# Halving the contraction of the responses' argument products: pairs of 64 rows in two banks instead of full products

## The chip, the cores and the metric

The kernel runs on one core of a Trainium2 chip. The metric is the device time of one execution in microseconds (us), the median of the runs shown. A profile of one execution gives the start, the length and the tiles of each instruction on five engines: TensorE (PE; its weight loads are PEld), VectorE (DVE), ScalarE (ACT), GpSimd (POOL) and SyncE (SP). "Form" below is the part of the array that a product uses, rows*columns: 128*128 is the whole, 64*128 a half of the rows, 128*32 a quarter of the columns.

## The reference

Two mixers of the same input are blended by a gate. One is a diagonal state-space convolution (L = 2048, D = 640, N = 128), the other a two-dimensional Fourier filter:

```python
dt = jnp.exp(log_dt)
A = -jnp.exp(log_A_real) + 1j * A_imag
C = (C_real + 1j * C_imag) * dt[:, None]
P = jnp.exp((A * dt[:, None])[:, :, None] * pos[None, None, :])
K = 2.0 * jnp.einsum("dn,dnl->dl", C, P).real
y = irfft(rfft(u) * rfft(K))[:L] + u * D_skip
b = irfft2(rfft2(x) * W)
g = sigmoid((x * gate_w).sum(-1))
out = g * y + (1 - g) * b
```

The change lies in the way to K, the convolution's response: 640 channels x 2048 positions, each a sum over 128 modes.

## The kernel before, in words

A position is split as l = 64 j + a, so that exp(A dt l) is a product of one factor for j (32 values) and one for a (64 values). Then K of a channel is a small matrix product over the 128 modes. The exponents and the angles of these factors (their "arguments") are linear in j and a, and a product makes them out of the parameters and a table.

`phase_p` (L233) prepares four parameters per channel and mode, each split into two float32r parts, and stores them as 8 rows per channel. `phase_b` (L602) goes through 40 tiles t of 16 channels. The stationary operand `pars[t]` has 128 rows, (channel x, parameter row), and 128 columns, the modes. The moving operands are tables that hold, for channel x, numbers in that channel's 8 rows and zeros elsewhere:

- `mags(t)` (L633): three products of 512 columns with `rm` (16 channels x 96), each into a bank p_e of a pool of two; ScalarE takes the exponential of each into the tile e (L639, L641).
- `phases(t)` (L644): two products of 512 columns with `rp` (2 x 16 channels x 32) into p_p, a bank of the same pool; ScalarE rounds (L652), VectorE subtracts (L653), which leaves q.
- `trig(t)` (L656): four sines of 512 columns on ScalarE. `prods(t)` (L671): x on VectorE (L676 to L678), y on GpSimd (L681, L683).
- `kgen(t)` (L685): 32 small products in column quarters, form 128*32, into p_k, two instructions each (float32 goes through the array twice; the float32r products of `mags` and `phases` are one instruction each). K goes to memory (L706).

Tiles go in groups of five: five `mags`, then five times `phases` and `trig`; `prods` and `kgen` follow a tile behind.

`merge` (L164) interleaves phase_b with another stream by weights that each generator yields. That stream is first `phase_a` (the transforms of the input: p_s, form 128*64, L336 and L349), then the spectral branch (L445 on): transposes p_t (L503), row transforms p_d (L519, L520), p_eo (L552) and p_i (L566), all of form 128*128 except in the last, half-size step, then the first transform of K (phase_c). `phase_d` (L769) ends the kernel. The recorded instructions are ordered once more, engine by engine, by the framework's scheduler, which looks at which operands and banks it expects to be free; the built order is therefore not the written one. On the chip each engine goes through its own instructions in that built order.

At the kernel's start two products of zeros (p_w, L379) run before the first data have landed. `phase_p` issues the loads of `rm` and `rp` (L317, L318) from GpSimd's queue.

Of the kernel before, what the change touches and what calls it, by code (L numbers as in the profile page):

```python
# [25 lines left out]
MAGIC = 12582912.0  # L26
# [22 lines left out]
A_ORDER = [*range(31, -1, -1), *range(32, 64)]  # L49


def _tables():
# [27 lines left out]
    k = np.array(POS_K)  # L80
    a = np.arange(64)
# [36 lines left out]


    j = np.arange(32)  # L120
    rp = np.zeros((8, 16, 2, 16, 32))
    rm = np.zeros((8, 16, 16, 96))
    for x in range(16):
        rp[0:2, x, 0, x] = j + 0.5
        rp[0:2, x, 1, x] = 64 * j + 31.5
        rp[2:4, x, 1, x] = 1.0
        rm[4:6, x, x, 0:64] = A_ORDER
        rm[4:6, x, x, 64:96] = 64 * j
        rm[6:8, x, x, 64:96] = 1.0
    f = lambda x: np.ascontiguousarray(x, dtype=np.float32)  # L130
    return {"t_c1": f(c1), "t_w2": f(w2), "t_w3": f(w3), "t_td": f(td),
            "t_rp": f(rp.swapaxes(0, 1).reshape(128, 1024)), "t_rm": f(rm.swapaxes(0, 1).reshape(128, 1536))}


def _lay_out(u, log_a, a_i, c_r, c_i, log_dt, d_skip, w_r, w_i, gate_w):
# [49 lines left out]
def body(tc, A, out):  # L185
    nc = tc.nc
    T = Ctx()
    with ExitStack() as top:
# [24 lines left out]
        with ExitStack() as cctx:  # L213
            def left():
                with ExitStack() as ctx:
                    T.bc = ctx.enter_context(tc.tile_pool(name="b_c", reuse_waits="tile", bufs=1))
                    T.rm = T.bc.tile([128, 1536], F32R, name="rm")
                    T.rp = T.bc.tile([128, 1024], F32R, name="rp")
# [135 lines left out]
def phase_a(tc, A, T):  # L354
# [3 lines left out]
    with ExitStack() as ctx:  # L358
# [15 lines left out]

        V.memset(lg[:, :, :], 0.0)
        z = lg.rearrange("p x a -> p (x a)")
        p = ps.tile([128, 512], F32, tag="ps", name="p_w")
        for _ in range(2):
            P.matmul(p[:, :], z[:, 0:128], z, start=True, stop=True)  # L379

        def copy(dst, src):

# [219 lines left out]
def phase_b(tc, A, T, ctx):  # L602
# [29 lines left out]

    def mags(t):  # L633
        e = es[t] = ep.tile([128, 16, 96], F32, tag="e", name="e")
        ef = e.rearrange("p d i -> p (d i)")
        for c in range(0, 1536, 512):
            p = ps.tile([128, 512], F32, tag="ps", name="p_e")
            with after(T.pin):
                P.matmul(p[:, :], pars[t], rm[:, c:c + 512], start=True, stop=True)  # L639
            with after(st.trig):  # L640
                st.exp = S.activation(ef[:, c:c + 512], p[:, :], AF.Exp)  # L641
            yield 0.2

    def phases(t, r):  # L644
        q = wt.tile([128, 2, 16, 32], F32, tag="w", name="q")
        qf = q.rearrange("p v d i -> p (v d i)")
        r.q = qf
        for c in range(0, 1024, 512):
            p = ps.tile([128, 512], F32, tag="ps", name="p_p")
            P.matmul(p[:, :], pars[t], rp[:, c:c + 512], start=True, stop=True)  # L650

            S.activation(qf[:, c:c + 512], p[:, :], AF.Copy, bias=MAGIC)  # L652
            V.scalar_tensor_tensor(out=qf[:, c:c + 512], in0=qf[:, c:c + 512], scalar=MAGIC, in1=p[:, :], op0=ALU.subtract, op1=ALU.subtract)  # L653
            yield 0.22

    def trig(t, r):  # L656
# [324 lines left out]
```

## Time and profile before

| what | value |
|---|---|
| median of 3 runs | 605.09 us (603.9 to 607.54) |
| profiled execution, span from first to last instruction | 605.9 us, the only time given for it |
| share of the span: TensorE, VectorE, ScalarE, GpSimd | 89%, 82%, 60%, 43% |
| exponentials of p_e, 120 of 128x512 | 602 ns each |
| roundings of p_p, 80 of 128x512 | 591 ns each |
| subtractions of p_p on VectorE, 80 of 128x512 | 680 ns each |
| mean granted TensorE clock | 0.963 |

How to read the rows that follow. A row of the busy time by stage has the stretch, its length, then busy time and number of instructions of each engine, the mean granted clock, the DMA share and the GB/s. A row of a group has the line, the engine, the operation, what it writes and reads, the shape, and how many; behind the bar the busy time and the mean length in ns; behind the second bar the engine's idle time just before them. A row of the timeline has the start, the length (of several instructions: from the first's start to the last's end), the engine, the line, the operation and how many. Matmuls overlap in the array, so the length of one holds the way through it; what a product costs is read from the starts of what comes before and behind.

### The profile page before, as it was taken

The numbers are of one execution on the slowest core, as the hardware profiler recorded it, in microseconds if no ns is written. First come the engines' busy times: TensorE is split into PE (matmuls) and PEld (weight loads), VectorE is DVE, ScalarE is ACT, GpSimd is POOL, SyncE is SP. The second block draws the span as 40 slices with busy tenths as digits, with TensorE's granted clock in tenths as the row PEclk, the third lists the DMA queues.
The fourth block names the chain that finished last, engine by engine and source line by source line (L and its number), as shares of the span: only waits on it lengthen the run. The fifth ranks groups of instructions, "written<-read, shape, count | busy, mean of one in ns | idle before, by whom it ended". The sixth has DMA issues, their size and how long they took to land. (4 is left out here: it accounts for less than half of the span.)

```text
span 605.9 us, 16674 instructions
## 1 busy us (share of the span) xinstructions
PE 537.6 (89%) x7084; PEld 409.0 (68%) x7084; DVE 496.4 (82%) x748; ACT 364.5 (60%) x659; POOL 263.0 (43%) x246
## 2 busy tenths in 40 slices
PE   9598979988989989989889989898969999999875
PEld 7586647766766667666667676656859877787651
DVE  5971597598899998999998899879397696995965
ACT  4556775476857777899697897798712322232120
POOL 4931153054346344444515344416253447547533
PEclk9999999999979997999897999999998999999979
DMA  8777203235612321243250232006684989879767
GB/s 342 292 283 264 90 2 130 92 133 196 245 45 66 100 85 41 79 125 125 67 140 22 55 96 110 29 23 212 212 346 146 364 274 287 313 254 322 241 211 269
DMA packets 48082, 101.96 MB, mean 168 GB/s; under 512 B 3316, under 2 KB 32776, under 8 KB 46248
## 3 DMA queue, kind: packets, MB, share of 16 engines
q1 hardware_dynamic: 24888, 67.74, 32.1%
q10 hardware_dynamic: 20080, 22.52, 11.9%
q0 software_dynamic: 3040, 10.65, 5.3%
q8 instruction: 55, 0.90, 0.6%
q14 instruction: 19, 0.16, 0.1%
HBM read 60.91 MB, written 39.98 MB: 167 GB/s over the span
## 5 line engine op out<-in xcount | busy, mean ns | idle before, releaser
L349 PE MATMUL p_s<-t,w 128*64 128x160 f32 x1056 | 91.6, 311 | 11.2 <-ACT ut L383 6.0
L681 POOL TENSOR_TENSOR y<-e,sc 128x512 f32<-128x512 f32 x40 | 55.4, 1384 | 89.2 <-DVE x L676 46.7
L349 PEld LDWEIGHTS p_s<-t,w 128*64 128x64 f32 x1056 | 75.9, 137 | 22.3 <-ACT ut L383 6.6
L641 ACT ACTIVATE e<-p_e 128x512 f32<-128x512 f32 x120 | 68.6, 602 | 23.6 <-PE p_e L639 21.4
L683 POOL TENSOR_TENSOR y<-e,sc 128x512 f32<-128x512 f32 x40 | 55.5, 1388 | 44.9 <-ACT sc L667 32.0
L696 PE MATMUL p_k<-x,y 128*32 128x64 f32 x2560 | 63.0, 227 | 11.2 <-POOL y L681 6.1
L696 PEld LDWEIGHTS p_k<-x,y 128*32 128x32 f32 x2560 | 45.2, 112 | 39.6 <-issue 24.2
L552 PE MATMUL p_eo<-td,pmt 107*128 107x321 f32 x204 | 67.5, 450 | 3.9 <-ACT pmt L506 3.9
L337 ACT COPY t<-p_s 128x512 f32<-128x512 f32 x40 | 24.5, 621 | 69.0 <-PE p_s L336 45.5
L653 DVE SCALAR_TENSOR_TENSOR q<-q,p_p 128x512 f32<-128x512 f32 x80 | 53.4, 680 | 13.5 <-ACT q L652 13.3
L639 PE MATMUL p_e<-rm,par 128*128 128x512 f32 x120 | 58.9, 520 | 5.2 <-ACT e L641 3.7
L803 POOL TENSOR_TENSOR t<-ma 64x320 f32<-64x320 f32 x32 | 27.9, 873 | 64.2 <-DVE ma L798 54.8
L652 ACT ACTIVATE q<-p_p 128x512 f32<-128x512 f32 x80 | 46.4, 591 | 6.6 <-PE p_p L650 6.2
L552 PEld LDWEIGHTS p_eo<-td,pmt 107*128 107x128 f32 x204 | 37.7, 194 | 18.4 <-ACT pmt L506 6.4
L678 DVE TENSOR_TENSOR x<-e,cx 128x1024 f32<-128x1024 f32 x40 | 48.5, 1212 | 1.9 <-ACT cx L669 1.9
L817 PE MATMUL p_i<-t,w 128*64 128x160 f32 x528 | 45.1, 308 | 4.4 <-POOL t L804 3.4
L336 PE MATMUL p_s<-c,kt 128*64 128x128 f32 x640 | 44.3, 277 | 3.9 <-DVE mb L799 2.0
L336 PEld LDWEIGHTS p_s<-c,kt 128*64 128x64 f32 x640 | 39.5, 138 | 12.2 <-issue 6.9
L650 PE MATMUL p_p<-rp,par 128*128 128x512 f32 x80 | 43.3, 546 | 4.6 <-DVE q L653 4.5
L819 ACT COPY s<-p_i 128x640 f32<-128x640 f32 x32 | 21.8, 693 | 38.8 <-PE p_i L817 38.7
L817 PEld LDWEIGHTS p_i<-t,w 128*64 128x64 f32 x528 | 39.1, 141 | 8.9 <-POOL t L804 4.0
L798 DVE TENSOR_TENSOR ma<-p_s,us 128x640 f32<-128x640 f32 (+1 forms) x36 | 28.2, 784 | 20.3 <-PE p_s L349 13.3
(153 smaller groups left out, 1186.4 us busy)
## 6 DMA issues: line engine op xcount, KB each, us to landing
u_d<-ut SPq DMA_DIRECT2D x32, 320.0 KB, 3.2
us<-u_d ACTq DMA_DIRECT2D x16, 640.0 KB, 6.0
s_d<-s ACTq DMA_DIRECT2D x15, 640.0 KB, 6.7
t<-s_d SPq DMA_DIRECT2D x14, 640.0 KB, 5.7
ww<-in_w_l SPq DMA_DIRECT2D x8, 642.0 KB, 3.8
ue<-u_d SPq DMA_DIRECT2D x8, 640.0 KB, 4.1
k_d<-kt SPq DMA_DIRECT2D x4, 1280.0 KB, 8.7
kt<-k_d SPq DMA_DIRECT2D x8, 640.0 KB, 5.9
```

Of the source, the lines that this page charges most:

```text
L336: nc.tensor.matmul(p[64 * ri:64 * ri + 64, j, :], src(i + j), e1[ri], start=True, stop=True)
L349: ins = nc.tensor.matmul(p[64 * j:64 * j + 64, i, 160 * ri:160 * ri + 160], w2[:, x, 64 * ri:64 * ri + 64], t1[:, x // 2 if x < 32 else K0 ...
L552: P.matmul(p[:, :E], st.pmt[:DC, c, w, j, :], tv[:DC, w, c, :], start=c == 0, stop=c == 2)
L639: P.matmul(p[:, :], pars[t], rm[:, c:c + 512], start=True, stop=True)
L641: st.exp = S.activation(ef[:, c:c + 512], p[:, :], AF.Exp)
L652: S.activation(qf[:, c:c + 512], p[:, :], AF.Copy, bias=MAGIC)
L653: V.scalar_tensor_tensor(out=qf[:, c:c + 512], in0=qf[:, c:c + 512], scalar=MAGIC, in1=p[:, :], op0=ALU.subtract, op1=ALU.subtract)
L678: V.tensor_tensor(out=x[:, 0].rearrange("p d (h j) -> p d h j", h=2), in0=e[:, :, 0:64].rearrange("p d (h j) -> p d h j", h=2), in1=cx.uns ...
L681: ins = G.tensor_tensor(out=y[:, 1], in0=e[:, :, 64:96], in1=sc[:, 0], op=ALU.mult)
L683: G.tensor_tensor(out=y[:, 0], in0=e[:, :, 64:96], in1=sc[:, 1], op=ALU.mult)
L696: P.matmul(st.pb[32 * r:32 * r + 32, o, :], y[:, ri, 4 * qq + JR[r], :], x[:, ri, 4 * qq + JR[r], :], start=t % 2 + qq + 1 - ri == 0, stop ...
L817: T.mm = P.matmul(p[x:x + 64, i // 2, 160 * (i % 2):160 * (i % 2) + 160], T.w3[:, k0 + h + i, x:x + 64], t2[:, h + i, :], start=True, stop ...
```

## The change

The tables are cut to what half of the rows needs. Channels 0 to 7 of a tile lie in rows 0 to 63 and channels 8 to 15 in rows 64 to 127, so `rp` shrinks from 1024 to 512 columns: rows 0 to 63 hold the table of the lower channels and rows 64 to 127 that of the upper. `phases` becomes two products of 64 rows and 512 columns, one with each half of the rows, into two banks taken at the same time. `mags` becomes one such pair (512 of each half's 768 columns) and one full product of 512 columns that holds the remaining 256 of both halves. So the number of products stays, three and two a tile; 160 of the 200 now have the form 64*128. ScalarE and VectorE do the same instructions on views with two runs of 256 for those columns. The tables in memory shrink from 768 and 512 KB to 512 and 256 KB. The two products of zeros at the start become 40 small ones in the forms 64*64, 64*32 and 32*64, into three banks.

```diff
     for x in range(16):
-        rp[0:2, x, 0, x] = j + 0.5
-        rp[0:2, x, 1, x] = 64 * j + 31.5
-        rp[2:4, x, 1, x] = 1.0
-        rm[4:6, x, x, 0:64] = A_ORDER
+        rp[0:2, x, 0, x % 8] = j + 0.5
+        rp[0:2, x, 1, x % 8] = 64 * j + 31.5
+        rp[2:4, x, 1, x % 8] = 1.0
+        rm[4:6, x, x % 8, 0:64] = A_ORDER
...
+    rest = np.zeros((8, 2, 8, 2, 256))
+    for h in range(2):
+        rest[:, h, :, h] = rm[:, 8 * h:8 * h + 8, 512:]
+    rm = np.concatenate([rm[:, :, :512], rest.reshape(8, 16, 512)], 2)
...
-        p = ps.tile([128, 512], F32, tag="ps", name="p_w")
-        for _ in range(2):
-            P.matmul(p[:, :], z[:, 0:128], z, start=True, stop=True)
+        pw = [ps.tile([128, 512], F32, tag="ps", name="p_w") for _ in range(3)]
+        for k, w, n in ((64, 64, 3), (64, 32, 2), (32, 64, 2)):
+            for i in range(n):
+                for r in range(min(3, 128 // k)):
+                    for x in range(0, 128, w):
+                        a = slice(k * r, k * r + k)
+                        P.matmul(pw[r][x:x + w, 160 * i:160 * i + 160], z[a, x:x + w], z[a, 0:160], start=True, stop=True)
...
-        for c in range(0, 1536, 512):
-            p = ps.tile([128, 512], F32, tag="ps", name="p_e")
-            with after(T.pin):
-                P.matmul(p[:, :], pars[t], rm[:, c:c + 512], start=True, stop=True)
-            with after(st.trig):
-                st.exp = S.activation(ef[:, c:c + 512], p[:, :], AF.Exp)
-            yield 0.2
+        pq = [ps.tile([128, 512], F32, tag="ps", name="p_e") for _ in range(2)]
+        with after(T.pin):
+            for h in range(2):
+                x = slice(64 * h, 64 * h + 64)
+                P.matmul(pq[h][:, :], pars[t][x], rm[x, 0:512], start=True, stop=True)
+        with after(st.trig):
+            for h in range(2):
+                st.exp = S.activation(ef[:, h, 0:512], pq[h][:, :], AF.Exp)
+        yield 0.4
+        p = ps.tile([128, 512], F32, tag="ps", name="p_e")
+        P.matmul(p[:, :], pars[t], rm[:, 512:1024], start=True, stop=True)
+        with after(st.trig):
+            st.exp = S.activation(ef[:, :, 512:768], p.rearrange("p (h i) -> p h i", h=2), AF.Exp)
+        yield 0.2
...
-        for c in range(0, 1024, 512):
-            p = ps.tile([128, 512], F32, tag="ps", name="p_p")
-            P.matmul(p[:, :], pars[t], rp[:, c:c + 512], start=True, stop=True)
+        pq = [ps.tile([128, 2, 256], F32, tag="ps", name="p_p") for _ in range(2)]
+        for h in range(2):
+            x = slice(64 * h, 64 * h + 64)
+            P.matmul(pq[h].rearrange("p v i -> p (v i)"), pars[t][x], rp[x], start=True, stop=True)
+        for h in range(2):
+            S.activation(qv[:, h], pq[h][:, :, :], AF.Copy, bias=MAGIC)
+            V.scalar_tensor_tensor(out=qv[:, h], in0=qv[:, h], scalar=MAGIC, in1=pq[h][:, :, :], op0=ALU.subtract, op1=ALU.subtract)
             yield 0.22
```

What the built order makes of it is seen on TensorE at three places. Line numbers moved: the pair of `mags` is L649, its full product L655, the pair of `phases` L668; p_eo is L552 before and L561 now, p_k L696 and L714, p_s L349 and L354, L336 and L341. The two tiles of a pair have numbers that follow each other.

The first place is the first two tiles of `mags`, beside phase_a. Before:

```order
L639 MATMUL p_e_756<-rm_73,par_753 128x512
L639 MATMUL p_e_759<-rm_73,par_753 128x512
L349 MATMUL p_s2_766<-t1_486,w2_68 64x160 x3
L639 MATMUL p_e_762<-rm_73,par_753 128x512
L349 MATMUL p_s2_766<-t1_486,w2_68 64x160
```

Now:

```order
L649 MATMUL p_e_796<-rm_73,par_793 128x512
L649 MATMUL p_e_797<-rm_73,par_793 128x512
L354 MATMUL p_s2_806<-t1_526,w2_68 64x160 x3
L655 MATMUL p_e_802<-rm_73,par_793 128x512
L354 MATMUL p_s2_806<-t1_526,w2_68 64x160
```

Here the pair stands together, with the full product behind other work; the neighbours have the form 128*64 both times.

The second place is a run of `mags` inside the spectral branch's p_eo. Before:

```order
L552 MATMUL p_eo_3204<-td_2016,pmt_3088 128x321
L639 MATMUL p_e_3146<-rm_73,par_2782 128x512
L639 MATMUL p_e_3197<-rm_73,par_2782 128x512
L552 MATMUL p_eo_3204<-td_2016,pmt_3088 128x321
L696 MATMUL p_k_3210<-x_3047,y_3048 32x64
L639 MATMUL p_e_3200<-rm_73,par_2782 128x512
```

Now:

```order
L649 MATMUL p_e_3237<-rm_73,par_2822 128x512
L561 MATMUL p_eo_3244<-td_2056,pmt_3128 128x321
L649 MATMUL p_e_3238<-rm_73,par_2822 128x512
L561 MATMUL p_eo_3244<-td_2056,pmt_3128 128x321
L714 MATMUL p_k_3250<-x_3087,y_3088 32x64
L655 MATMUL p_e_3246<-rm_73,par_2822 128x512
```

The two halves, p_e_3237 and p_e_3238, have a p_eo between them. Before, p_e and p_eo had the same form.

The third place is one tile's `phases` among p_eo. Before:

```order
L552 MATMUL p_eo_3443<-td_2016,pmt_3381 128x321
L650 MATMUL p_p_3405<-rp_74,par_2782 128x512
L552 MATMUL p_eo_3443<-td_2016,pmt_3381 128x321
L650 MATMUL p_p_3421<-rp_74,par_2782 128x512
L552 MATMUL p_eo_3496<-td_2016,pmt_3381 128x321
```

Now:

```order
L561 MATMUL p_eo_3483<-td_2056,pmt_3421 128x321
L668 MATMUL p_p_3445<-rp_74,par_2822 128x512
L561 MATMUL p_eo_3483<-td_2056,pmt_3421 128x321
L668 MATMUL p_p_3446<-rp_74,par_2822 128x512
L561 MATMUL p_eo_3536<-td_2056,pmt_3421 128x321
```

The places in the order are the same, but the products between the p_eo now have another form.

More of the change, by code (lines that the diff above doesn't have):

```diff
@@ L216, in left @@
                     T.bc = ctx.enter_context(tc.tile_pool(name="b_c", reuse_waits="tile", bufs=1))
-                    T.rm = T.bc.tile([128, 1536], F32R, name="rm")
-                    T.rp = T.bc.tile([128, 1024], F32R, name="rp")
+                    T.rm = T.bc.tile([128, 1024], F32R, name="rm")
+                    T.rp = T.bc.tile([128, 512], F32R, name="rp")
                     yield from phase_p(tc, A, T)
```

16 lines of the change are left out of this document (8 added, 8 removed).

## The prediction

> **What bounds the kernel now.** I read the page's shares first, then the busy time by stage, and last the timeline of TensorE around single products.
>
> ```profile
> span 605.9 us, 16674 instructions
> PE 537.6 (89%) x7084; PEld 409.0 (68%) x7084; DVE 496.4 (82%) x748; ACT 364.5 (60%) x659; POOL 263.0 (43%) x246
> ...
> core 0: us, PE busy (x) PEld busy (x) DVE busy (x) ACT busy (x) POOL busy (x), PEclk, DMA share, GB/s
> 0.00:55.00 55.00, 44.41 (x712) 39.22 (x712) 35.79 (x49) 29.93 (x57) 28.87 (x28) 0.97 0.83 302
> 55.00:158.00 103.00, 92.90 (x1537) 66.12 (x1538) 76.97 (x129) 69.13 (x119) 32.88 (x28) 0.98 0.33 113
> 158.00:430.00 272.00, 247.62 (x2944) 181.84 (x2942) 249.37 (x372) 219.61 (x409) 118.20 (x101) 0.95 0.29 91
> 430.00:606.00 176.00, 152.66 (x1898) 121.81 (x1894) 134.25 (x199) 45.82 (x76) 83.08 (x89) 0.97 0.82 277
> ...
> 500.00:550.00 50.00, 46.95 (x580) 38.15 (x580) 40.52 (x59) 14.87 (x24) 27.90 (x31) 1.00 0.87 285
> ```
>
> The responses (phase_b) run from 55 to 430 us. Up to 158 us they share the array with phase_a; there TensorE is busy 92.90 of 103 us and VectorE only 76.97. From 158 us they share it with the spectral branch; there TensorE (247.62 of 272 us, 91.0%) and VectorE (249.37) are both nearly full, and TensorE is idle for 24.4 us in all. Only TensorE gets other work by this change.
>
> The waits of that second stage, cut to TensorE and to VectorE (the first rows), show what the idle time is made of:
>
> ```profile
> PE p_eo L552 <- ACT pmt L506: 3.9, 4, 2.2
> PE p_p L650 <- DVE q L653: 2.8, 3, 2.3
> PE p_k L696 <- POOL y L681: 2.7, 3, 2.0
> PE p_t L503 <- DVE pm L542: 2.6, 1, 2.6
> ...
> DVE q L653 <- ACT q L652: 10.8, 10, 2.9
> ```
>
> These are single waits of about 2 us on other engines, not one engine that is always late. The products that change are these two groups:
>
> ```profile
> L639 PE MATMUL p_e<-rm,par 128*128 128x512 f32 x120 | 58.9, 520 | 5.2 <-ACT e L641 3.7
> L650 PE MATMUL p_p<-rp,par 128*128 128x512 f32 x80 | 43.3, 546 | 4.6 <-DVE q L653 4.5
> ```
>
> **What a product costs, and what a change of form costs.** A "form" is the rows*columns in front of the shape. Same form on both sides (p_p between two p_d):
>
> ```profile
> 325.50 0.44 PE L520 MATMUL p_d<-td,ft 65*128 65x161 f32 x2
> 325.67 0.50 PE L650 MATMUL p_p<-rp,par 128*128 128x512 f32 x1
> 326.01 0.43 PE L519 MATMUL p_d<-td,ft 128*128 128x160 f32 x2
> 326.28 0.44 PE L520 MATMUL p_d<-td,ft 65*128 65x160 f32 x2
> ```
>
> Starts count here, since durations hold the way through the array. A pair of p_d instructions takes 326.28 - 326.01 = 0.27 us; from 325.50 to 326.01 a pair and a p_p take 0.51; so p_p costs 0.24. Two p_e in a row say the same (0.73 against 0.50 for one, so 0.23 more), and their two loads take 0.30 against 0.19 for one: a load occupies 0.11 us and is hidden.
>
> ```profile
> 151.91 0.73 PE L639 MATMUL p_e<-rm,par 128*128 128x512 f32 x2
> ...
> 151.91 0.30 PEld L639 LDWEIGHTS p_e<-rm,par 128*128 128x128 f32 x2 [0.24 <-issue]
> ```
>
> Between instructions that use 64 rows (the short transposes at the end of the spectral branch), with a change of form before and behind:
>
> ```profile
> 410.04 0.30 PE L503 MATMUL p_t<-c,pm 64*107 64x64 f32 x1
> 410.28 0.49 PE L650 MATMUL p_p<-rp,par 128*128 128x512 f32 x1
> 410.70 0.87 PE L503 MATMUL p_t<-c,pm 64*107 64x64 f32 x7
> ```
>
> One p_t takes (0.87 - 0.30)/6 = 0.095 us; from 410.04 to 410.70 is 0.66; so p_p costs 0.57 there, 0.33 more, or 0.17 for each change of form. [...] So a row form costs a change like any other. [...] I take 0.20 beside the spectral products (long streams, hidden loads) and 0.17 beside the others. Lower end: 0.19 us (0.42 - 0.23, the leaving side alone) for two, 0.095 each.
>
> **The change, part by part.**
>
> *Changes of form.* The built order is not the written one: other work is put between the halves of most pairs. Counted over the whole order, 19 of the 80 pairs stand together (14 of 40 for the magnitudes, 5 of 40 for the phases); 6 of the 19 stand before the spectral branch's first transpose (at 157.7 us in this trace), 13 behind it. A lone half product still streams 512 columns, so it saves nothing. Neighbours with a different form go from 120 to 131 in the first stage and from 158 to 299 in the second, since the spectral branch's products are 128*128 and every half product among them is now a change in and a change out. Sum: first stage 11 x 0.17 = +1.9 us, second 141 x 0.20 = +28.2 us of TensorE time.
>
> *Pairs that stand together.* No row shows two row halves at once. Products in four column strips do run side by side:
>
> ```profile
> 289.89 1.10 PE L696 MATMUL p_k<-x,y 128*32 128x64 f32 x64
> ```
>
> [...] I take the row halves to do likewise: the second costs nothing, -0.23 us each, 6 x 0.23 = -1.4 and 13 x 0.23 = -3.0 us. The other end is 0. [...]
>
> *What passes to the end.* Second stage: 247.6 + 28.2 - 3.0 = 272.8 us of work in 272 us. No long stretch of this trace gets TensorE busier than 46.95 of 50 us (94%, the last row of the first block); at 94% the stage takes 290.2 us, +18.2. Ends: at today's 91%, 299.8 us, +27.8; at 100%, +0.8. I take 94%, as part of the waits of 2 us will be filled and VectorE has little more room than TensorE. First stage: 1.9 - 1.4 = +0.5.
>
> *ScalarE, VectorE, waits.* Their instructions keep number and size (three exponentials of 512 columns, two roundings, two subtractions a tile), in views with two runs; no cost, as both keep their engines' pace. The pair needs both banks of its pool at once, where one at a time sufficed; a half whose bank is still being read is what the order moves back, so that this cost shows as the lone halves above.
>
> *Start.* The probe products are 40 of 160 columns, two instructions each, against 4 instructions of 512:
>
> ```profile
> 1.44 3.78 PE L379 MATMUL p_w<-lg 128*128 128x512 f32 x4 [1.44 <-DVE lg L375]
> 5.15 1.12 PE L336 MATMUL p_s<-c,u 128*64 128x128 f32 x8
> ...
> 15.00:30.00 15.00, 8.56 (x144) 7.52 (x140) 14.93 (x11) 8.75 (x17) 14.84 (x13) 0.93 0.75 290
> ```
>
> At p_w's pace (3.78/4 = 0.95 us for 512 columns) 160 columns take 0.30. If all tiles of a form run together, the 12, 16 and 12 products are 3, 2 and 2 rounds of two instructions, 14 x 0.30 = 4.2 us, about as now; if only column tiles do, 6, 4 and 6 rounds, 32 x 0.30 = 9.6 us, some 6 us later. TensorE idles 6.4 us between 15 and 30 us, which covers most: 0, upper end +3. The tables shrink by 512 KB, at 302 GB/s 1.7 us of transfers: 0, lower end -1.7.
>
> Sum: 605.9 + 18.2 + 0.5 = 624.6 for the profiled execution, whose span is 0.8 over the median of 605.1: 623.8 us.
>
> **The rivals.**
>
> *Pairs do not overlap even when together*, so the change does not do what it says: no -3.0 and -1.4; 275.8/0.94 = 293.4, +21.4, and +1.9: 628.4 us. Against it: the p_k row. 0.12.
>
> *Everything passes on*: 0.215 a change, no overlap, 91%: (247.6 + 30.3)/0.91 = 305.4, +33.4, with +2.4 and +3: 605.1 + 38.8 = 643.9 us. 0.12.
>
> *The waits take it*: at 0.095 a change the second stage holds 247.6 + 13.4 - 3.0 = 258.0 us, which at 95% is 272: 605 us. It decides if the lower price holds and the 24.4 us of idle time fill. 0.12.
>
> *The clock stays up*:
>
> ```profile
> 172.00:175.00 3.00, 0.39 (x3) 0.09 (x1) 3.00 (x7) 1.69 (x3) 0.86 (x1) 0.97 0.60 219
> 175.00:182.00 7.00, 6.87 (x27) 4.82 (x28) 7.00 (x13) 3.05 (x5) 4.17 (x3) 0.53 0.01 2
> ```
>
> After a 2.6 us wait the granted clock falls to about a half for 7 us. At a mean of 0.95 the second stage spends 272 x 0.05 x 2 = 27 us at half clock, half of it (13.6) lost. If fuller queues end all such waits: (272.8 - 13.6)/0.94 = 275.7, +3.7 and +0.5: 609 us. Against it: the waits are on other engines. 0.08.
>
> *Faster, by VectorE*: if VectorE bounds the second stage and both halves landing together end its 10.8 us of waits for q, 605.1 - 10.8 = 594 us; it decides only if TensorE's additions stay under its 24.4 us of idle time, and 35 of the 40 phase pairs stand apart. 0.05.
>
> *Faster, all 80 pairs at the price of one*: 54 pairs behind 158 us give 12.4 us, (247.6 - 12.4)/0.91 = 258.5, -13.5, and the 26 before 6.0: 585.6 us. [...] The rows at 410 us speak against it for halves that stand apart. 0.04.
>
> **How the numbers follow.** The likeliest case has 0.47 and, with its own bounds (price 0.17 to 0.215, 92 to 96%), reaches from 613 (268.6/0.96) to 633 us (274.9/0.92). A measurement tells 1%, about 6 us, from no change. Slower by more: 0.47 + 0.12 + 0.12 = 0.71; within 1%: 0.12 + 0.08 = 0.20; faster: 0.05 + 0.04 = 0.09. The range runs from 603 (the waits take it, with the lighter transfers) to 642 (nearly everything passes on).
>
> **What would show it.** Price: a half product alone among p_eo should cost 0.6 to 0.7 us from start to start beyond its neighbours, against 0.24. Overlap: in a pair that stands together the second product starts within a few hundredths of the first and both end together. Passing on: TensorE busy 94% between the spectral branch's first transpose and the last product, that stage near 290 us, everything behind 430 us moved as a block. The forecast is wrong if halves among 128*128 products show no gap before their load, or if the half-clock stretches vanish.

## The result

| kernel | time, us | lowest to highest | ratio to before |
|---|---|---|---|
| before | 605.57 | 603.9 to 607.54 | |
| after | 655.59 | 654.52 to 657.51 | 1.083 (1.0798 to 1.0862) |

The change makes the kernel 50 us slower. The forecast was 623.8 us, at most 642: the sign was right, the size was not. The profiled execution of after took 657.51 us, 1.9 over the median; its span is 655.7. (Executions that took over 1.5% longer than the fastest of their kernel beside them are left out of the times and ratios of the experiments: two each of the kernel that streams all halves twice and of the same-form control, and one each of the kernel with pairs together in early tiles, of the one with the magnitudes together, and of before.)

The busy time by stage of after, cut where the same work ends (its columns are those of the rows shown before the prediction):

```profile
0.00:55.00 55.00, 44.03 (x780) 40.11 (x780) 34.91 (x47) 28.73 (x55) 28.72 (x28) 0.97 0.83 298
55.00:166.00 111.00, 101.00 (x1544) 71.37 (x1545) 78.10 (x130) 69.59 (x121) 32.28 (x28) 0.89 0.30 102
166.00:480.00 314.00, 286.83 (x2966) 189.41 (x2966) 249.78 (x372) 221.28 (x410) 110.32 (x101) 0.89 0.25 81
480.00:656.00 176.00, 150.73 (x1876) 118.96 (x1872) 134.56 (x199) 46.14 (x76) 83.05 (x89) 0.98 0.81 274
```

The start and the last stage (176 us both times) are as before. The first stage grew from 103 to 111 us, the second from 272 to 314, and they hold the whole loss. VectorE and ScalarE do the same work in them (249.37 and 249.78 us in the second). TensorE's busy time grew by 8.1 and 39.2 us, and the column behind POOL, the mean granted clock, fell from 0.98 and 0.95 to 0.89 in both.

The same from 55 us to the last product of the responses' arguments, split at the first p_t of the spectral branch: before, then after.

```profile
55.00:157.70 102.70, 92.60 (x1534) 65.83 (x1534) 76.97 (x129) 68.83 (x118) 32.88 (x28) 0.98 0.33 113
157.70:420.80 263.10, 240.24 (x2805) 175.49 (x2807) 242.37 (x363) 211.35 (x395) 112.58 (x96) 0.95 0.29 90
```

```profile
55.00:165.80 110.80, 100.80 (x1543) 71.17 (x1543) 78.10 (x130) 69.39 (x120) 32.28 (x28) 0.89 0.30 102
165.80:470.70 304.90, 278.63 (x2731) 182.24 (x2734) 243.06 (x363) 213.10 (x395) 104.65 (x96) 0.88 0.24 78
```

Together 365.8 became 415.7 us, 49.9 more. TensorE's idle time went from 33.0 to 36.3 us (10.1 + 22.9, then 10.0 + 26.3): none of it was filled. Its busy time went from 332.8 to 379.4. In the records of the granted clock of both traces, which begin at 7.6 and 6.9 us, a stretch has either 1.00 or 0.50, so the time at half clock can be added up: 30.7 us of this part before, 95.6 after.

The groups of the changed products, and the waits of VectorE for what ScalarE makes of them (busy time and mean ns, then the idle time before and its releaser):

```profile
L668 PE MATMUL p_p<-rp,par 64*128 64x512 f32 x80 | 43.8, 567 | 8.8 <-DVE q L671 8.8
L649 PE MATMUL p_e<-rm,par 64*128 64x512 f32 x80 | 34.2, 505 | 1.9 <-DVE q L671 1.9
L655 PE MATMUL p_e<-rm,par 128*128 128x512 f32 x40 | 21.6, 541 | 2.9 <-ACT e L652 2.9
L671 DVE SCALAR_TENSOR_TENSOR q<-q,p_p 128x512 f32<-128x512 f32 x80 | 53.0, 681 | 28.2 <-ACT q L670 26.5
```

VectorE's group before:

```profile
L653 DVE SCALAR_TENSOR_TENSOR q<-q,p_p 128x512 f32<-128x512 f32 x80 | 53.4, 680 | 13.5 <-ACT q L652 13.3
```

The products' own groups did not grow (43.3 us before for p_p, 43.8 now; 58.9 before for p_e, 34.2 + 21.6 now). The time is not in them, but between them and their neighbours. VectorE waits 26.5 us for q, 13.3 before; in the second stage the waits are 24.0 against 10.8.

What one half product costs is read from starts. On TensorE of after, among p_eo at full clock:

```profile
446.81 0.50 PE L655 MATMUL p_e<-rm,par 128*128 128x512 f32 x1
447.15 0.70 PE L561 MATMUL p_eo<-td,pmt 107*128 107x321 f32 x2
447.78 0.50 PE L668 MATMUL p_p<-rp,par 64*128 64x512 f32 x1
448.21 0.81 PE L561 MATMUL p_eo<-td,pmt 107*128 107x321 f32 x2
448.95 0.50 PE L668 MATMUL p_p<-rp,par 64*128 64x512 f32 x1
```

From 447.78 to 448.95 stand one half and two p_eo, 1.17 us; two p_eo take 0.54 (0.70 - 0.43 = 0.27 for one more), so the half takes 0.63, where the full product took 0.24. A change in and a change out cost 0.39 us.

The same at half clock, among p_i of after, and below it a like place of before at full clock:

```profile
364.13 1.44 PE L575 MATMUL p_i<-qq,w 128*128 128x320 f32 x2
365.49 0.79 PE L668 MATMUL p_p<-rp,par 64*128 64x512 f32 x1
366.22 1.44 PE L575 MATMUL p_i<-qq,w 128*128 128x320 f32 x2
367.58 0.79 PE L668 MATMUL p_p<-rp,par 64*128 64x512 f32 x1
```

```profile
355.78 0.70 PE L566 MATMUL p_i<-qq,w 128*128 128x320 f32 x2
356.08 0.63 PE L650 MATMUL p_p<-rp,par 128*128 128x512 f32 x1
356.55 0.70 PE L566 MATMUL p_i<-qq,w 128*128 128x320 f32 x2
356.84 0.63 PE L650 MATMUL p_p<-rp,par 128*128 128x512 f32 x1
```

Two p_i and a product took 0.77 us (355.78 to 356.55); the clock alone would make that 1.54; it is 2.09 (364.13 to 366.22), so each change costs about 0.28 us here. And why is the clock at a half? The busy time by stretches of after, around this place:

```profile
344.80:348.20 3.40, 0.70 (x19) 0.45 (x19) 2.25 (x4) 1.50 (x3) 3.23 (x5) 1.00 0.02 5
348.20:372.10 23.90, 23.90 (x147) 15.70 (x150) 12.59 (x20) 11.08 (x22) 6.24 (x6) 0.50 0.13 39
372.10:375.50 3.40, 3.40 (x87) 2.69 (x76) 3.03 (x5) 3.40 (x7) 1.91 (x2) 1.00 0.20 61
```

TensorE had little to do for 3.4 us (0.70 of 3.40; it waited 3.01 us for GpSimd's y), and the clock fell. Then the page calls it busy for 23.90 of 23.90 us, and the clock stays at a half for all of that. "Busy" here also counts what the changes of form take: in the p_i rows above at most 1.54 of 2.09 us, 74%, are columns on their way in. The 23.90 us are seven stretches of 3.41 us, the length of the shortest whole spell at half clock in this trace. TensorE is busy for the whole of each by the profile's column, and the clock stays at a half behind six of them and rises behind the seventh. How full the seven are is in the last section.

### The profile page after: what moved, and what is told of

Same layout as the page of the kernel before. It is cut to its first block, busy times and chain, and to the rows that moved or that the text cites. A ratio compares the mean times of both kernels' runs of the same rounds, so it can differ in the third digit from the quotient of the medians.

```text
span 655.7 us, 16815 instructions
## 1 busy us (share of the span) xinstructions
PE 582.6 (89%) x7160; PEld 419.8 (64%) x7160; DVE 497.4 (76%) x748; ACT 365.7 (56%) x659; POOL 254.4 (39%) x246
## 4 chain that ended last, share of the span: by engine, by line
PE 59%; DVE 20%; ACT 7%; DMA 6%; issue 5%; POOL 1%; SPq 0%; ACTq 0%; DVEq 0%; POOLq 0%
PE p_eo L561 11%; PE p_s L354 7%; PE p_s L341 6%; PE p_k L714 5%; PE p_p L668 4%; PE p_e L649 4%; PE p_i L835 4%; PE p_t L512 3%; PE p_i L575 3%; PE p_d L528 3%; PE p_d L529 3%; DVE t L822 2%; DVE ma L816 2%; PE p_c L914 2%; PE p_e L655 2%
## 5 line engine op out<-in xcount | busy, mean ns | idle before, releaser
L354 PE MATMUL p_s<-t,w 128*64 128x160 f32 x1056 | 92.9, 315 | 11.7 <-ACT ut L392 6.3
L354 PEld LDWEIGHTS p_s<-t,w 128*64 128x64 f32 x1056 | 76.6, 139 | 22.7 <-ACT ut L392 7.2
L701 POOL TENSOR_TENSOR y<-e,sc 128x512 f32<-128x512 f32 x40 | 52.0, 1301 | 85.9 <-ACT sc L685 46.9
L699 POOL TENSOR_TENSOR y<-e,sc 128x512 f32<-128x512 f32 x40 | 51.6, 1291 | 75.8 <-DVE x L694 63.0
L561 PE MATMUL p_eo<-td,pmt 107*128 107x321 f32 x204 | 77.2, 505 | 3.0 <-ACT pmt L515 3.0
L671 DVE SCALAR_TENSOR_TENSOR q<-q,p_p 128x512 f32<-128x512 f32 x80 | 53.0, 681 | 28.2 <-ACT q L670 26.5
L714 PE MATMUL p_k<-x,y 128*32 128x64 f32 x2560 | 64.5, 236 | 10.9 <-POOL y L699 5.6
L714 PEld LDWEIGHTS p_k<-x,y 128*32 128x32 f32 x2560 | 47.7, 118 | 40.9 <-issue 28.3
L652 ACT ACTIVATE e<-p_e 128x512 f32<-128x512 f32 x80 | 45.5, 599 | 19.0 <-PE p_e L649 18.5
L561 PEld LDWEIGHTS p_eo<-td,pmt 107*128 107x128 f32 x204 | 38.9, 211 | 24.2 <-issue 11.1
L670 ACT ACTIVATE q<-p_p 128x512 f32<-128x512 f32 x80 | 45.6, 589 | 13.1 <-PE p_p L668 13.1
L821 POOL TENSOR_TENSOR t<-ma 64x320 f32<-64x320 f32 x32 | 27.9, 873 | 61.0 <-DVE ma L816 61.0
L668 PE MATMUL p_p<-rp,par 64*128 64x512 f32 x80 | 43.8, 567 | 8.8 <-DVE q L671 8.8
L696 DVE TENSOR_TENSOR x<-e,cx 128x1024 f32<-128x1024 f32 x40 | 48.5, 1212 | 2.2 <-ACT cx L687 2.1
L835 PE MATMUL p_i<-t,w 128*64 128x160 f32 x528 | 42.6, 300 | 4.4 <-POOL t L822 3.4
L341 PE MATMUL p_s<-c,kt 128*64 128x128 f32 x640 | 43.2, 274 | 3.4 <-DVE mb L817 2.0
L341 PEld LDWEIGHTS p_s<-c,kt 128*64 128x64 f32 x640 | 38.1, 136 | 11.7 <-issue 7.5
L341 PE MATMUL p_s<-c,u 128*64 128x128 f32 x640 | 43.2, 283 | 0.0
L835 PEld LDWEIGHTS p_i<-t,w 128*64 128x64 f32 x528 | 36.7, 137 | 9.2 <-POOL t L822 4.0
L528 PE MATMUL p_d<-td,ft 128*128 128x161 f32 (+3 forms) x144 | 38.5, 358 | 4.4 <-ACT ft L517 4.3
```

The source lines that it names most:

```text
L341: nc.tensor.matmul(p[64 * ri:64 * ri + 64, j, :], src(i + j), e1[ri], start=True, stop=True)
L354: ins = nc.tensor.matmul(p[64 * j:64 * j + 64, i, 160 * ri:160 * ri + 160], w2[:, x, 64 * ri:64 * ri + 64], t1[:, x // 2 if x < 32 else K0 ...
L528: P.matmul(v, st.ft[:, c, x, :nl], tab[0], start=True, stop=False)
L561: P.matmul(p[:, :E], st.pmt[:DC, c, w, j, :], tv[:DC, w, c, :], start=c == 0, stop=c == 2)
L668: P.matmul(pq[h].rearrange("p v i -> p (v i)"), pars[t][x], rp[x], start=True, stop=True)
L670: S.activation(qv[:, h], pq[h][:, :, :], AF.Copy, bias=MAGIC)
```

## The experiments

The theories, in the order in which they came up: *form* (each change costs 0.2 us of TensorE, which passes on whole), *clock* (more time at half clock), *banks* (the pair takes two banks at once, and the engines behind lose their rhythm). The table has all kernels (one was run once more, for a second profile): the time and ratio, the changes of form counted over the whole built order, the time at half clock of a whole execution (2 x (1 - mean granted clock) x span, median of the executions compared), and in the profiled one TensorE's idle time from 55 us to the last product of the arguments. Each diff is cut to the lines that matter; "..." stands for what goes with them (tables, views, the reading instructions). None of the kernels leaves out a result; where products are repeated or tiny ones added, they go to the same bank and the last one holds.

| kernel | us | ratio | changes | half clock, us | idle, us |
|---|---|---|---|---|---|
| before | 605.5 | | 288 | 46 | 33.0 |
| after | 655.6 | 1.083 (1.080 to 1.086) | 442 | 107 | 36.3 |
| two banks, full rows | 620.1 | 1.025 (1.021 to 1.030) | 289 | 58 | 38.8 |
| phases as after | 646.6 | 1.069 (1.063 to 1.074) | 367 | 115 | 34.3 |
| magnitudes as after | 617.4 | 1.021 (1.016 to 1.025) | 364 | 49 | 30.9 |
| all pairs together | 632.2 | 1.045 (1.041 to 1.050) | 371 | 88 | 46.0 |
| half rows, one bank | 653.8 | 1.082 (1.077 to 1.087) | 454 | 102 | 35.0 |
| after, halves streamed twice | 650.8 | 1.077 (1.070 to 1.084) | 417 | 58 | 26.0 |
| phases: two banks, full rows | 618.4 | 1.025 (1.019 to 1.031) | 285 | 63 | 36.6 |
| phases: half rows, one bank | 645.4 | 1.068 (1.063 to 1.073) | 372 | 104 | 34.5 |
| the same, streamed twice | 649.2 | 1.072 (1.064 to 1.080) | 361 | 86 | 29.9 |
| pairs together, early tiles | 611.2 | 1.009 (1.005 to 1.012) | 281 | 56 | 38.6 |
| magnitudes together | 623.7 | 1.030 (1.022 to 1.037) | 347 | 56 | 40.4 |
| tiny products, other form | 624.6 | 1.029 (1.021 to 1.036) | 384 | 65 | 27.9 |
| tiny products, same form | 619.2 | 1.019 (1.010 to 1.029) | 285 | 52 | 27.1 |

The repeats of before beside these runs had medians from 604.7 to 607.3 us.

### Two banks with all rows, and half rows with one bank

After, with all 128 rows and the wide tables, each channel group still in a bank of its own:

```diff
...
-                P.matmul(pq[h][:, :], pars[t][x], rm[x, 0:512], start=True, stop=True)
+                P.matmul(pq[h][:, :], pars[t], rm[:, 512 * h:512 * h + 512], start=True, stop=True)
...
-            P.matmul(pq[h].rearrange("p v i -> p (v i)"), pars[t][x], rp[x], start=True, stop=True)
+            P.matmul(pq[h].rearrange("p v i -> p (v i)"), pars[t], rp[:, 512 * h:512 * h + 512], start=True, stop=True)
...
```

> The changed kernel with its two banks at a time, its views and its probe products, but every product takes all 128 rows again (tables as before, columns regrouped by halves): no half-row products, 289 changes of form in the built order against 288 before and 442 in the changed kernel. Theory 'form' (the 50 us come from changes of form, with the clock falling in their wake): within 6 us of before, 600 to 612 us, half-clock time between 55 us and the last product near the 31 us of before. Rival 'banks' (taking two banks at once makes TensorE and VectorE wait): at least 630 us, with VectorE's waits for the rounded q near the 26 us of the changed kernel.

And the other half of the change, half rows, but one bank taken, read and given back before the next:

```diff
...
-        pq = [ps.tile([128, 2, 256], F32, tag="ps", name="p_p") for _ in range(2)]
         for h in range(2):
+            p = ps.tile([128, 2, 256], F32, tag="ps", name="p_p")
             x = slice(64 * h, 64 * h + 64)
-            P.matmul(pq[h].rearrange("p v i -> p (v i)"), pars[t][x], rp[x], start=True, stop=True)
-        for h in range(2):
-            S.activation(qv[:, h], pq[h][:, :, :], AF.Copy, bias=MAGIC)
+            P.matmul(p.rearrange("p v i -> p (v i)"), pars[t][x], rp[x], start=True, stop=True)
+            S.activation(qv[:, h], p[:, :, :], AF.Copy, bias=MAGIC)
...
```

> All half-row products of the changed kernel, but asked for one bank at a time as before (product, ScalarE, yield; then the other half), so that no pair stands together: 454 changes of form, 166 more than before. Theory 'form alone': 166 x 0.32 = +53 us, about 659 us. Theory 'form and banks add up' (full rows in two banks cost 14 us): 606 + 50 - 14 = 642 us. Theory 'clock' (a change of form costs little by itself, but the time in which nothing streams keeps the array at half clock): whatever the sum, more than half of the added time is half-clock time times 0.5.

Banks alone cost 14 us (620.1), half rows alone 49 (653.8), both 50. So the half rows make the loss, and beside them the banks add nothing that can be told from zero. With half rows in one bank, half of the added half-clock time (102 against 46 us) makes 28 of the 49 us, as 'clock' had it. The two banks with full rows met neither forecast: the 14 us were not expected by form, as the number of changes is that of before (289), and they are less than banks had said; half-clock time and idle time are both somewhat higher (58 against 46 us, 38.8 against 33.0). Why, was not followed up for all rows.

### Phases or magnitudes

Each as after, with the other as before:

```diff
...
+            x = slice(64 * h, 64 * h + 64)
+            P.matmul(pq[h].rearrange("p v i -> p (v i)"), pars[t][x], rp[x], start=True, stop=True)
...
```

> Only the phases' products as pairs of 64 rows (5 of 40 pairs stand together), magnitudes and start as before: 367 changes of form, 79 more than before. Theory 'form' at 50/154 = 0.32 us a change: +25 us, about 630 us. Rival 'banks': the phases hold the waits for q, so nearly all of the loss, 640 us or more.

```diff
...
+                x = slice(64 * h, 64 * h + 64)
+                P.matmul(pq[h][:, :], pars[t][x], rm[x, 0:512], start=True, stop=True)
...
```

> Only the magnitudes' products as pairs (16 of 40 stand together), phases and start as before: 364 changes of form, 76 more than before. Theory 'form': 76 x 0.32 less 16 x 0.23 = +21 us, about 626 us. Rival 'banks': the small rest, under 618 us.

The phases alone cost 41 us against their own repeats of before, the magnitudes 11, at nearly the same number of added changes (79 and 76). That is the first blow to form as the only cause: 0.52 us a change in the one, 0.15 in the other. What differs with it is the clock: the half-clock time went up by 69 us with the phases, by 3 with the magnitudes. Of neighbouring half products, 1 of 6 went side by side with the phases and 11 of 16 with the magnitudes, which is at most ten times 0.23 us. By their numbers both runs came as banks had said (over 640, under 618); that banks are not the reason is shown by the next pair.

The phases in two banks with full rows, and with half rows in one bank:

```diff
...
-            P.matmul(p[:, :], pars[t], rp[:, c:c + 512], start=True, stop=True)
+            P.matmul(pq[h].rearrange("p v i -> p (v i)"), pars[t], rp[:, 512 * h:512 * h + 512], start=True, stop=True)
...
```

> Only the phases take two banks at once, with full rows, all else as before: no half rows, 285 changes of form. Theory 'banks' (the 14 us of full rows in two banks belong to the phases, whose rounded q VectorE then waits for): about 620 us. Rival (they come from the magnitudes or the order at the start): within 6 us of before.

```diff
...
-            P.matmul(p[:, :], pars[t], rp[:, c:c + 512], start=True, stop=True)
+            P.matmul(p.rearrange("p v i -> p (v i)"), pars[t][x], rp[x], start=True, stop=True)
...
```

> Only the phases have half rows, one bank at a time as before, all else as before: 372 changes of form, 84 more than before. Theory 'form alone', 0.32 us each: +27 us, 633 us. Theory 'form and banks add up': 646.6 less the 14 us of two banks, also 633 us. If the phases' loss is all banks: within 6 us of before. Theory 'clock': the time moves with the half-clock time, at 0.5 us each, plus 0.1 us a change.

618.4 and 645.4 us: the same split again, 14 us for the banks, 41 for the half rows, and 41 for both. The second is over the 633 us of 'form alone' and of the sum; by 'clock', 58 us more at half clock at 0.5 each and 84 changes at 0.1 make 37 of the 41.

### All pairs together

The first half waits until both banks have been read, so that nothing comes between the halves; in the built order 74 of 80 pairs stand together.

```diff
...
+    def free(ins):
+        for x in st.used:
+            if x is not None:
+                tc.add_manual_dep(ins.ins, x.ins.name, SYNC, reason="pair")
...
-            P.matmul(pq[h].rearrange("p v i -> p (v i)"), pars[t][x], rp[x], start=True, stop=True)
+            ins = P.matmul(pq[h].rearrange("p v i -> p (v i)"), pars[t][x], rp[x], start=True, stop=True)
+            if h == 0:
+                free(ins)
...
```

> The changed kernel, but the first half of a pair also waits until the second half's bank is free, so that in the built order 74 of 80 pairs stand together (19 before): 371 changes of form, 83 more than the kernel before, 71 fewer than the changed one. Theory 'form': 83 x 0.32 less 74 x 0.23 = +10 us, about 615 us, and the two halves start within 0.02 us of each other in nearly all pairs. Rival 'banks': waiting for both banks makes it worse than the changed kernel, over 655 us.

TensorE of this kernel, around a pair of the magnitudes:

```profile
299.81 0.44 PE L528 MATMUL p_d<-td,ft 128*128 128x161 f32 x2
300.18 0.50 PE L658 MATMUL p_e<-rm,par 64*128 64x512 f32 x2
300.61 0.54 PE L529 MATMUL p_d<-td,ft 65*128 65x161 f32 x2
300.99 0.44 PE L528 MATMUL p_d<-td,ft 128*128 128x160 f32 x2
301.26 0.43 PE L529 MATMUL p_d<-td,ft 65*128 65x160 f32 x2
```

Both halves lie in 0.50 us, and the pair takes 0.43 from its start to the next p_d, no more than a lone half. In all 73 neighbouring pairs in the trace the halves start 3 or 4 ns apart. The overlap is real, and with 371 changes the kernel is 23 us faster than after. It is still 26 us slower than before, so both forecasts missed (615 us, over 655). TensorE is idle for 13.0 us more than before (46.0 against 33.0), and half-clock time is still 88 us. The idle time does not stand in front of the pairs: TensorE's waits for the readers of the arguments' banks are 9.2 us in all, 8.2 before. What grew is p_k's wait for GpSimd's y, here before and then this kernel:

```profile
PE p_k L696 <- POOL y L681: 6.1, 6, 2.0
```

```profile
PE p_k L729 <- POOL y L714: 14.0, 12, 3.1
```

Whether waiting for both banks brought that about was not tested.

Two cheaper versions, from before: pairs together for the first 15 tiles of the magnitudes and 11 of the phases only, whose neighbours are phase_a's p_s; and for all magnitudes, with the phases as before (the second diff is against the first).

```diff
...
+    NM, NQ = 15, 11
...
+                    ins = P.matmul(pq[h][:, :], pars[t][x], rm[x, 768 * h:768 * h + 512], start=True, stop=True)
+                    if h == 0:
+                        free(ins)
...
```

> The kernel before, with pairs of 64 rows only in the tiles whose products stand beside phase_a (15 tiles of magnitudes, 11 of phases), where the neighbours use column strips and the form changes anyway; the first half waits for both banks, so that 25 of 26 pairs stand together: 281 changes of form against 288. Theory 'form and clock': 25 x 0.23 + 7 x 0.1 = 6.5 us less, about 599 us, half-clock time as before (31 us). Rival 'banks' (two banks at a time cost by themselves, wherever they are taken): 26 of 80 pairs of the 14 us, +5 us less the 6, no change from before.

```diff
-    NM, NQ = 15, 11
+    NM, NQ = 40, 0
```

> Only the magnitudes as pairs, all 40, the first half waiting for both banks, so that 35 of 40 stand together (16 in the earlier run with the magnitudes alone, 617.4 us): 347 changes of form, 59 more than before. Theory 'form and clock': 59 x 0.1 - 35 x 0.23 = -2 us of work, half-clock time within 10 us of before: 600 to 611 us. Rival 'banks': the wait for both banks costs as it does with all pairs together, 620 us or more.

Neither beats before: 0.9% and 3.0% slower, so 'form and clock' missed both times; 'banks' came near in the first and right in the second, by the number. In the first, all 25 pairs in the trace ran side by side, and TensorE's work in the first stage fell:

```profile
55.00:158.10 103.10, 87.56 (x1538) 63.66 (x1534) 78.23 (x130) 67.89 (x117) 32.27 (x28) 0.95 0.32 107
```

87.56 us against 92.60, but the stage is as long as before (102.7 and 103.1): the 5 us saved became waits, 15.5 us of idle time against 10.1. The argument products' waits for a bank grew from 2.7 to 4.8 us, p_k's for its operands and its bank from 6.1 to 10.0. Among the first are:

```profile
PE p_e L661 <- ACT e L658: 2.4, 5, 1.3
...
PE p_e L653 <- ACT e L663: 1.4, 2, 0.7
```

A likely reason for these, not tested by itself: with two banks in the pool, whoever waits for both gives away the overlap of the next product with the reading of the last.

### Streaming twice

If half-clock time comes from too few streamed columns, more of them should lower it, although they are more work. Each half product of the phases twice into the same bank (from the one-bank kernel), and each half of after twice:

```diff
-            P.matmul(p.rearrange("p v i -> p (v i)"), pars[t][x], rp[x], start=True, stop=True)
+            for _ in range(2):
+                P.matmul(p.rearrange("p v i -> p (v i)"), pars[t][x], rp[x], start=True, stop=True)
```

> The phases alone with half rows, one bank at a time (the run before: 645.4 us), each half product issued twice into the same bank: 361 changes of form instead of 372, 80 more streams of 0.21 us, 17 us more work. Theory 'work': 645 + 17 - 1 = 661 us. Theory 'clock' (the array goes back to full clock only after a stretch of 3.4 us that is nearly all streaming, and each change of form takes streaming away): half-clock time between 55 us and the last product falls from 88.7 us by at least 20, time 652 us or less.

> The changed kernel with every half-row product issued twice into the same bank, so that the same changes of form (417 in the built order) stand beside twice the streaming: 160 more products of 0.21 us, 34 us more work for TensorE. Theory 'work' (changes of form and streams are simply summed): 655 + 34 - 8 = about 680 us. Theory 'clock': a larger share of each 3.4 us streams, the half-clock time between 55 us and the last product falls well below the 95.6 us of the changed kernel (to under 60 us) and gives back half of that: 665 us or less.

> The kernel with every half-row product issued twice once more, for a profile, since the one taken lies 10 us over that kernel's median of 655.9. Theory 'clock': in an execution near 651 to 656 us the half-clock time between 55 us and the last product is under 75 us (95.6 in the changed kernel). Theory 'work': it is about 95 us, and the added streaming has gone into TensorE's idle time (36 us in the changed kernel), which would then be near zero.

The forecasts took 0.21 us for a repeated product, the author's estimate, which no run shows; measured is 0.23, for a full one beside its like (151.91 us in before, 0.73 less 0.50). At that price the phases' 80 more products are 18.4 us of work; the time rose by 3.8 (645.4 to 649.2; the intervals of the ratios overlap), half-clock time fell from 104 to 86 us and idle time from 34.5 to 29.9. In the two profiles half-clock time from 55 us to the last product fell from 88.7 to 63.8 us, as 'clock' had forecast; the second stage of the one-bank phases, then of the same streamed twice:

```profile
159.70:459.10 299.40, 274.20 (x2733) 185.38 (x2734) 242.28 (x363) 213.06 (x395) 104.14 (x96) 0.87 0.25 80
```

```profile
158.90:455.00 296.10, 272.33 (x2738) 184.06 (x2741) 238.87 (x361) 212.01 (x392) 107.09 (x96) 0.90 0.25 81
```

If half-clock time costs its half, which is the most it can, 18 us less give 9 us back, with the idle time 13.6, and 4.8 of the 18.4 are left.

All halves of after: 37 us more work at 0.23 us each, 25 changes fewer (5 us at 0.20). The five executions took 650.8, 650.9, 661.0, 667.9 and 668.6 us, with 56, 60, 77, 97 and 99 us at half clock; those of after took 655 to 658 us with 106 to 114. So the 650.8 us of the table are the two fastest, and it is not shown that this kernel is faster than after; but all five are under the 680 us of 'work'. The two profiles are of the two slowest, with about 89 us at half clock between 55 us and the last product, hardly less than in after; there the expectation was missed, and no trace shows where the half-clock time came off in the others. So the phases speak for the clock; this kernel does so only by times and mean clocks, and its traces do not.

### The change of form by itself, with all rows

A tiny product (8 columns, form 128*32) ahead of each phase product, which keeps all its rows; and as a control the same in the form 128*128 (its diff is against the first):

```diff
+            P.matmul(p[0:32, 0:8], T.id[:, 0:32], T.id[:, 0:8], start=True, stop=True)
             P.matmul(p[:, :], pars[t], rp[:, c:c + 512], start=True, stop=True)
```

> The kernel before, full rows, one bank at a time, with a tiny product of 8 columns in the form 128*32 ahead of each of the 80 phase products, into the same bank, which the phase product then overwrites: 384 changes of form against 288 (372 where the phases alone had half rows, 645.4 us). Theory 'change of form': about as that run, 635 to 650 us, with half-clock time of 60 us or more between 55 us and the last product. Rival 'half rows' (the array counts half-used rows as idle, and the clock falls for that): under 618 us and half-clock time near the 31 us of before.

```diff
-            P.matmul(p[0:32, 0:8], T.id[:, 0:32], T.id[:, 0:8], start=True, stop=True)
+            P.matmul(p[:, 0:8], T.id, T.id[:, 0:8], start=True, stop=True)
```

> The same with the tiny product in the form 128*128, that of the phase products: 285 changes of form. Both theories: near before, 604 to 612 us, since 80 products of 8 columns add some 0.05 to 0.1 us each; more than that would be the price of the tiny product itself and has to be taken off the run beside it.

The time lies between the two forecasts. With 384 changes, 96 more than before and 12 more than the one-bank phases, it is 624.6, not 645.4 us, and the half-clock time 65, not 104. So changes of form alone do not make the loss: with the half rows kept to the phases, 21 us more come at fewer changes, along with 38 us more at half clock. The control is not clean, and over its forecast of 604 to 612 us: the tiny products cost 1.9% (1.0 to 2.9), about 12 us, without any added change of form (with two loads of 128 columns each), so that the 17 us of the first, against its own repeats of before, are not the price of 96 changes. Both kernels have less idle time than before (27.9 and 27.1 us), and the added loads and products are work.

## Why the prediction was wrong

*The number and the price of the changes: right.* 278 became 430 by the prediction's count; a lone half among p_eo takes 0.63 us, forecast 0.6 to 0.7, and 0.39 of it is the two changes, 0.20 each (the rows at 447 us). The forecast's 0.20 beside the spectral products, and the 0.215 of its upper bound and of a rival, were the author's estimate, which no trace of before shows; its rows at 410 us give 0.17, and those at 447 us of after the 0.20.

*Pairs together: right in the price, half as many as counted on.* Ten of 20 neighbouring pairs of halves in the trace of after start within 0.04 us of each other, such as these two between p_s, and in the kernel with all pairs together 73 of 73 do:

```profile
56.92 0.31 PE L354 MATMUL p_s<-t,w 128*64 128x160 f32 x2
57.15 0.51 PE L649 MATMUL p_e<-rm,par 64*128 64x512 f32 x2
57.59 0.36 PE L354 MATMUL p_s<-t,w 128*64 128x160 f32 x2
```

In the other ten the second half starts 0.17 us or more behind the first, in each some 50 ns after the end of the instruction that reads its bank. One of them:

```profile
228.03 0.43 PE L561 MATMUL p_eo<-td,pmt 107*128 107x321 f32 x1
228.39 0.71 PE L668 MATMUL p_p<-rp,par 64*128 64x512 f32 x2
229.02 0.81 PE L561 MATMUL p_eo<-td,pmt 107*128 107x321 f32 x2
```

Two halves take 0.71 us here, not 0.51: the exponential that reads the second's bank ends at 228.55 (227.95 and 0.60 long), and the second product starts at 228.60. The terms of -1.4 and -3.0 us were for 19 pairs; half of that came. This is small.

*What passes to the end: wrong.* The step "I take 94%, as part of the waits of 2 us will be filled" failed. TensorE was busy 278.63 of 304.9 us, 91.4%, as before (240.24 of 263.1, 91.3%). The work was spread over more time, and so were the waits; none was filled. The 94% came from a single stretch of 50 us behind the responses (200 to 250 us, inside the second stage, reaches the same, 46.99 of 50): what one stretch reaches, the whole stage with its waits did not. The engines that TensorE waits for are themselves behind it: VectorE's waits for q rose as shown above, and ScalarE's for p_p (over the span) from 6.2 us to 13.1:

```profile
L670 ACT ACTIVATE q<-p_p 128x512 f32<-128x512 f32 x80 | 45.6, 589 | 13.1 <-PE p_p L668 13.1
```

At 91.3% the prediction's own 272.8 us give 298.8 in place of 290.2: 8.6 us of the miss.

*The clock: taken as 0, the mis-sized term.* "The clock stays up" was the only place where it stood, and with the opposite sign. Half-clock time between 55 us and the last product went from 30.7 to 95.6 us. If all of that were streaming it would cost half, 32 us (two p_i take 1.44 us at half clock, 0.70 at full, in the rows at 364 and 355 us). The work of other engines does not stretch with it (in after the 25 roundings of p_p that start at half clock take 586 ns in the mean, the other 55 take 590), nor do waits for it, so this is an upper limit; over the 95 executions kept, those of one kernel differ by 0.23 us per us at half clock, which would make 15 (a fit, and no lower limit). The forecast of +18.7 and the 8.6 leave 22.7 us of the 50, under the limit. Of these, 7.6 lie in the first stage, forecast at +0.5 us and measured at +8.1 (102.7 to 110.8): its half-clock time went from 3.4 to 23.9 us. How the 22.7 divide between the clock and anything else was not measured. That the clock is a cause, and not only a companion, rests on the phases' repeated products (18 us more work, less time at half clock, and a time that is up by only 3.8 us), and on the tiny products, where more changes than in the one-bank phases came with 38 us less at half clock and a time 21 us lower.

*The rest: right.* Behind the last product all moved as a block, the lighter tables and the probe products changed nothing (44.41 and 44.03 us of TensorE in the first 55). The rival "everything passes on" had the right direction at 643.9 us; it lacked the clock. The rivals in which VectorE, or pairs for the price of one, make it faster had no part: 10 pairs of 80 overlapped.

*What stays open.* Why phases lower the clock and magnitudes hardly do (69 and 3 us more at half clock); what the two banks cost with all rows (14 us); how much of the loss is the clock's; and what brings the clock back up. Whether it follows the rows that a product uses, beside its columns, was not shown: no run changes the rows alone, without changes of form.

## What to carry to other kernels

A product of half the rows among products of all rows costs its two changes of form, 0.39 us here against 0.23 for the product itself, and can pay only if its twin stands right beside it with its own bank already free; even with all pairs together no kernel here was faster than before. Before cutting a contraction, count in the built order how many pairs will be neighbours, and ask whether two banks will be free at that place (a pool of more than two was not tried). Where TensorE is near its limit, add up the half-clock time as a term of its own: in after the clock stayed at a half for 23.90 us in which the engine looks 100% busy, and the one-bank phases, with half rows and 372 changes, had 104 us at half clock where the tiny products, with all rows and 384 changes, had 65.

## What the runs showed of the hardware

In the traces of before and after, every spell at half clock from 15 us on is a multiple of 3.41 us (23.89, 17.07, 10.24, 6.83 and 3.41 in after; 10.24, 6.83 and 3.41 in before), but for the last of each, which the end cuts off.

There are 21 falls of the clock in the two from 15 us on (9 and 12), 19 rises (8 and 11), and 24 stretches of 3.41 us after which the half clock stayed (5 and 19). By the profile's column TensorE was busy for 0.00 to 0.63 of the 3.41 us ahead of a fall, for 0.99 or more of those ahead of a rise (but for one of 0.77, at 28 us in before), and for 0.32 to 1.00 of those after which the clock stayed down; 13 of these 24 were busy throughout. So a busy stretch went before a rise in some places and before more half clock in others.

Nor does the time in which columns enter the array tell the seven stretches of the 23.90 us above apart. An estimate of it, from 0.23 us for 512 columns of the argument products (151.91 us in before) and 0.27 us for 321 columns of p_eo, twice that at half clock, and products in column strips by the part of the columns that they use, gives shares of 0.69, 0.92, 0.89, 0.71, 0.78, 0.72 and 0.79: the clock stayed down behind the second and the third and rose behind the last, with 0.79, where 'clock' had asked for a stretch that is nearly all streaming.

A change of form costs 0.20 us at full clock (0.39 for two, the rows at 447 us) and about 0.28 at half (the rows at 364 us). Two row halves in free banks take the time of one (0.50 us for both, the rows at 300 us of the kernel with all pairs together).
